# A Conformer branch layer, forward and backward: stores and loads moved from SyncE's DMA queue to GpSimd's and ScalarE's

## The chip, the cores and the metric
The kernel runs as one launch on one core of a Trainium2 chip. The time is the device time of the core in microseconds. The engines are named as in the profile: PE (TensorE matmul) with PEld (its weight load), DVE (VectorE), ACT (ScalarE), POOL (GpSimd) and SP (SyncE, which computes nothing here and issues DMAs).

## The reference
The layer has an attention branch and a local branch over x of shape (2, 4000, 144) in bfloat16. The kernel must return the output and the gradients of x and of all seven weights for a given grad_out.

```
xa = layernorm(x);  q, k, v = split(xa @ w_qkv)
p  = softmax(q k^T / sqrt(144));  glob = (p @ v) @ w_att_out
u, g = split(gelu(xa @ w_mlp_in));  g = layernorm(g)
gc = depthwise conv of g over time, 5 taps (dw_csgu)
loc = (u * gc) @ w_mlp_out
m = concat(glob, loc);  m = m + depthwise conv of m, 5 taps (dw_merge)
out = x + m @ w_merge
returns: out, and the gradients of x, w_qkv, w_att_out, w_mlp_in,
         dw_csgu, w_mlp_out, dw_merge, w_merge
```

## The kernel before
A batch of 4000 tokens is held as 125 partitions by 32 blocks, token = partition * 32 + block, so that there are 64 row tiles of 125 tokens in the two batches. Weights are folded together at the start (the head), so the attention works with rows of xa instead of q, k and v.

**Attention.** `phase_att` goes over the 64 row tiles, several of them in flight. For row tile i, the query rows and the rows of the incoming gradient are projected and turned by a DMA transpose (`jit_tr`, qt<-qb, L1162). `quad` makes the scores S and the products dP against all 4000 tokens of the batch, 1000 columns at a time (L1181, L1188). The scores go to Pbuf with a running minimum of their negative (DVE, L1203) and through the exponential (ACT, L1209); dP is copied to Sbuf by ACT (L1219) and multiplied by P on DVE (L1220). Both are transposed by DMA, half a row tile at a time: PT<-Pbuf at L1213 and ST<-Sbuf at L1408, all issued by SP. `Y_half` multiplies PT with xa (L1230, PE); ACT scales the result to yn (L1243), which is stored to DRAM (Yn_d, L1244), and GpSimd forms QBs (L1252), an operand of the matmuls X (L1325). `Z_half` does the same with ST (L1269) and stores zn (Zn_d, L1274); zn is also transposed (zt<-zn, L1281). The matmuls X sum the gradient of xa into acc on DVE (L1332). yn has two buffers and zn two.

**Local branch.** `local_units` does the local branch and its gradient per batch in small units woven into the attention. GpSimd computes a reciprocal root rsr (L596), which DVE uses at L611, and a product l_w (L677). The product u*g is stored to DRAM (ug_d, L658), and a few rows at the borders are spilled and read back (held, keep, ring, L533 to L644). Towards the end of the first batch `prep_late` loads x and grad_out of the second (L430 to L445), normalises them with statistics that GpSimd finishes (rstd_x, L458), and fills the rest of the operands (XR<-R, L504). Rows of the first batch that are needed again are spilled by `spill_xa0` (xa_d, L2006, called at L1499) and `spill_acc0` (acc_d, L2007, called at L1335).

**Merge and weight gradients.** `Merge` reads Yn_d, Zn_d and ug_d back, turns them by DMA transposes (L1672), computes the output in `out_g` (matmuls L1717 and L1719, the addition of x on DVE at L1720, a store) and the gradient of x in `dx_b` (DVE L1743, ACT L1744, GpSimd L1746, a store). The tiles o_ and dxo come from a pool with two buffers. `Final` computes the weight gradients and stores them.

**Who issues what.** `move` and `load_tok` split a transfer of 125 partitions into 112 and 13, so each is two DMAs (L47 and L48, L42 and L43). In the kernel before, SP issues nearly every DMA, 943 in the order lists; GpSimd issues 15 loads of weights into the operands of the end (L71, L100, L101), and ACT a few loads at the start.

**The order.** `Planner` records all instructions. `plan` (L1086) chains those of each engine in an order written out by hand: ORDER holds for each engine a list of numbers, one for each instruction or group of up to 16 alike (PE 1392 entries, DVE 2501, Activation 1668, Pool 379, SP 943). DMA issues are entries of the engine that issues them. An engine works strictly in this order, so an instruction that waits holds back all those behind it on its engine.

Of the kernel before, what the change touches and what calls it, by code (L numbers as in the profile page):

```python
# [411 lines left out]
def prep_late(k, W, b, S, es, pst):  # L412
# [15 lines left out]
    def start():  # L428
        nc.gpsimd.memset(S.xa_aug[:, :, D:D + 1], 1.0)
        nc.sync.dma_start(S.R[80:96, :], k.R0[80:96, :])  # L430
        nc.sync.dma_start(S.R[112:128, :], k.R0[112:128, :])
        nc.gpsimd.memset(halo_t[0:32, 0:2, :], 0.0)
        nc.gpsimd.memset(halo_t[96:PB, 2:4, :], 0.0)
        nc.sync.dma_start(halo_t[1:PB, 0:2, :], gv[0:PB - 1, NB - 2:NB, :])
        nc.sync.dma_start(halo_t[0:PB - 1, 2:4, :], gv[1:PB, 0:2, :])

    def load_x(g):
        if g < 4:
            load_tok(k, xin, 8 * g, xv, 8 * g, 8 * g + 8, nc.sync)

    def load_go(*qs):
        for q in qs:
            if q < 8:
                GQ[q] = sp.tile([PB, 4, D], BF, tag="gq", name="gq", bufs=4)
                load_tok(k, GQ[q], 0, gv, 4 * q, 4 * q + 4, nc.sync)  # L445
# [52 lines left out]
    def xar(g):  # L498
        pr = pst()
        for bi in range(8):  # L500
            nc.tensor.transpose(pr[0:112, bi, 0:PB], S.xa_aug[:, 8 * g + bi, 32:D], W.ident[0:PB, 0:PB])
        nc.vector.tensor_copy(v8(S.R, 8 * g, 8)[96:112], pr[96:112, :, 0:PB])
        for c in (2 * g, 2 * g + 1):
            nc.sync.dma_start(S.XR[32 * (c % 4):32 * (c % 4) + DR, (c // 4) * CH:(c // 4 + 1) * CH], S.R[96:112, c * CH:(c + 1) * CH])  # L504
# [17 lines left out]
def local_units(k, W, b, S, A, es, DHT, ps_w, gw):  # L522
# [10 lines left out]
    nc.sync.dma_start(held[1][PB - 1:PB].rearrange("p a b c -> p (a b c)"), k.zdram[0:1, 0:4 * D])  # L533
# [81 lines left out]
    def e_dgc(g):  # L615
# [5 lines left out]
        if g == NG2 - 1:  # L621
            nc.sync.dma_start(ring[1:PB, :, 0:2, :], t[0:PB - 1])
            nc.sync.dma_start(held[0][:], t)
        if g == 0:
            nc.sync.dma_start(held[1][0:PB - 1], t[1:PB])

    def e_hold():
        for i in range(2):
            nc.sync.dma_start(ring[:, :, 8 + 2 * i:10 + 2 * i, :], held[i][:])
        nc.sync.dma_start(hgr[0][:, :, 0:D], keep[0][:])  # L630
        nc.sync.dma_start(dugr[0][:], keep[1][:])
        nc.sync.dma_start(gpr[0][:], keep[2][:])
# [5 lines left out]
    def e_gp(g):  # L638
        nc.vector.tensor_tensor(sq[:], z_[:], a_[:], op=ALU.mult)
        nc.vector.tensor_tensor(gpr[new(g)][:], sq[:], q_[:], op=ALU.add)  # L640
        if g == NG2 - 1:
            nc.sync.dma_start(keep[0][:], hgr[new(g)][:, :, 0:D])
            nc.sync.dma_start(keep[1][:], dugr[new(g)][:])
            nc.sync.dma_start(keep[2][:], gpr[new(g)][:])  # L644
# [8 lines left out]
    def gc_unit(g):  # L653
# [4 lines left out]
        nc.sync.dma_start(S.ug_d[:, G2 * g:G2 * g + G2, :], ug[:])  # L658
# [113 lines left out]
class Planner:  # L772

    ORDER = {
# [1432 lines left out]
```

## Time and profile before

| | |
|---|---|
| runs (us) | 1182.25, 1186.67, 1194.44 |
| median | 1186.67 us |
| profiled execution | 1190.94 us |
| its span, first to last instruction | 1189.2 us |
| granted TensorE clock, mean | 0.992 |
| PE busy | 1134.5 us, 95% |
| DVE busy | 1021.0 us, 86% |
| ACT busy | 913.0 us, 77% |
| POOL busy | 228.1 us, 19% |
| share of the 16 DMA engines | 81.4% for SP's queue, 167 GB/s in the mean |

The profile is one execution. "Busy" counts instructions that compute; the time in which an engine issues a DMA isn't counted, so POOL's 19% and ACT's 77% leave out what they issue. A line such as "PE yz L1230 <- DMA PT<-Pbuf" says that PE, about to write yz at line 1230, waited for the DMA that fills PT from Pbuf. SPq, ACTq and POOLq are the queues of those engines, and a time beside a DMA issue there is how long the queue stood at it, which includes its wait for the source where the two aren't told apart. The span has five stages: the head up to about 60 us, attention of the first batch to 440, the change of batches to 530, attention of the second batch to 1045, and the merge with the weight gradients to the end.

### The profile page before, as it was taken

The page shows a single profiled execution, that of the slowest core. Times are in us where ns is not written, and L with a number is a line of the kernel's source. Part 1 is how long each engine was busy: PE and PEld are TensorE (multiplying, and loading weights), DVE is VectorE, ACT ScalarE, POOL GpSimd, SP SyncE. Part 2 cuts the span into 40 slices and gives each one's busy share as a digit, 9 for nine tenths or more (in the row PEclk, how much of TensorE's full clock was granted, in tenths as well). Part 3 has the DMA queues.
Part 4 walks back from the last instruction along what each step waited for, and adds up shares of the span by engine and source line. Part 5 has one row for each costly group of instructions (what it writes and reads, how often), then busy time and mean ns, then how long its engine had stood idle before and what let it go on. Part 6 is the DMA issues. An engine that isn't in the chain of part 4 may idle for free. (4 is left out here: it accounts for less than half of the span.)

```text
span 1189.2 us, 36104 instructions
## 1 busy us (share of the span) xinstructions
PE 1134.5 (95%) x14389; PEld 880.8 (74%) x14389; DVE 1021.0 (86%) x3043; ACT 913.0 (77%) x1662; POOL 228.1 (19%) x383
## 2 busy tenths in 40 slices
PE   6999999999999889999999999999999999998898
PEld 3667777777777667777676777777777776898887
DVE  8579999999999989778799999999999985676555
ACT  5999888888998766678898888888889766453252
POOL 7111112111112123200011111111111020023441
PEclk9999999999999999999999999999999999999989
DMA  3778888899898999778998988878989889857643
GB/s 106 165 167 167 160 165 176 177 159 182 167 185 165 166 172 203 167 149 170 205 193 160 160 171 161 185 157 172 167 175 165 174 167 181 205 148 185 157 124 97
DMA packets 673144, 198.43 MB, mean 167 GB/s; under 512 B 648915, under 2 KB 666889, under 8 KB 672955
## 3 DMA queue, kind: packets, MB, share of 16 engines
q1 hardware_dynamic: 671846, 194.74, 81.4%
q8 instruction: 112, 1.84, 0.7%
q0 software_dynamic: 592, 1.18, 0.4%
q14 instruction: 56, 0.46, 0.1%
q10 hardware_dynamic: 538, 0.21, 0.1%
HBM read 24.45 MB, written 17.85 MB: 36 GB/s over the span
## 5 line engine op out<-in xcount | busy, mean ns | idle before, releaser
L1203 DVE TENSOR_SCALAR_CACHE_REDUCE Pbuf<-ps 125x1000 bf16<-125x1000 f32 x256 | 306.3, 1197 | 47.0 <-PE ps L1188 37.5
L1219 ACT CAST Sbuf<-ps 125x1000 bf16<-125x1000 f32 x252 | 252.3, 1001 | 101.5 <-PE ps L1188 81.7
L1209 ACT ACTIVATE Pbuf<-Pbuf,nm 125x1000 bf16<-125x1000 bf16 x256 | 284.9, 1148 | 7.7 <-DVE nm L1205 7.4
L1325 PE MATMUL X<-QBs,Sbuf 125*128 125x144 bf16 x2048 | 282.8, 226 | 0.8 <-ACT QBs L1248 0.4
L1325 PE MATMUL X<-QBs,Pbuf 125*128 125x144 bf16 x2048 | 281.5, 226 | 1.0 <-POOL QBs L1252 0.6
L1181 PE MATMUL ps<-xaT_m,qt 128*128 128x500 bf16 x1024 | 262.3, 376 | 6.7 <-DVE Pbuf L1203 4.9
L1325 PEld LDWEIGHTS <-Sbuf 125*128 125x128 bf16 x2048 | 198.4, 98 | 18.7 <-issue 18.3
L1325 PEld LDWEIGHTS <-Pbuf 125*128 125x128 bf16 x2048 | 200.1, 98 | 2.1 <-issue 1.6
L1220 DVE TENSOR_TENSOR Sbuf<-Sbuf,Pbuf 125x1024 bf16<-125x1024 bf16 x252 | 172.0, 687 | 8.0 <-ACT Pbuf L1209 5.4
L1230 PE MATMUL yz<-xa_aug,PT 125*128 125x145 bf16 x2048 | 151.1, 228 | 14.1 <-DMA PT<-Pbuf 13.2
L1269 PE MATMUL yz<-xa_aug,ST 125*128 125x144 bf16 x2048 | 151.4, 229 | 4.9 <-DMA ST<-Sbuf 4.6
L1230 PEld LDWEIGHTS <-PT 125*128 125x128 bf16 x2048 | 131.7, 98 | 29.4 <-DMA PT<-Pbuf 18.7
L1181 PEld LDWEIGHTS <-qt 128*128 128x128 bf16 x1024 | 92.0, 98 | 70.6 <-issue 9.6
L1269 PEld LDWEIGHTS <-ST 125*128 125x128 bf16 x2048 | 133.2, 98 | 14.7 <-issue 8.0
L1252 POOL TENSOR_TENSOR QBs<-g,g 125x144 bf16<-125x144 f32 x64 | 35.7, 558 | 451.1 <-ACT g L1251 293.9
L1332 DVE TENSOR_TENSOR acc<-X,acc 125x432 f32<-125x432 f32 (+1 forms) x204 | 110.1, 547 | 13.7 <-PE X L1325 13.0
L1188 PEld LDWEIGHTS <-qt 16*128 16x128 bf16 x1024 | 26.4, 91 | 110.2 <-issue 110.2
L1188 PE MATMUL ps<-XR,qt 16*128 16x500 bf16 x1016 | 100.4, 380 | 0.0
L1744 ACT ACTIVATE t<-t,dx_c,rstd_x 125x144 f32<-125x144 f32 x64 | 28.6, 500 | 50.7 <-DVE t L1743 45.6
L649 DVE TENSOR_TENSOR l_prod<-ring,Wc 125x720 bf16<-125x720 bf16 x128 | 66.0, 535 | 0.2
L677 POOL TENSOR_SCALAR l_w<-ring,nc,c 125x144 f32<-125x144 bf16 x64 | 30.7, 485 | 176.1 <-DVE nc L673 86.1
L1614 PE MATMUL Hps<-Yg,go_h 125*128 125x144 bf16 x640 | 55.9, 229 | 1.5 <-DMA Yg<-ug_d 1.5
(558 smaller groups left out, 1941.7 us busy)
## 6 DMA issues: line engine op xcount, KB each, us to landing
Yn_d<-yn SPq DMA_DIRECT2D x64, 35.2 KB
Zn_d<-zn SPq DMA_DIRECT2D x64, 35.2 KB
ug_d<-ugr SPq DMA_DIRECT2D x32, 70.3 KB
PT<-Pbuf SPq DMA_TRANSPOSE x126
ST<-Sbuf SPq DMA_TRANSPOSE x126
acc_d<-acc SPq DMA_DIRECT2D x4, 504.0 KB
go_h<-in_grad_out_dram SPq DMA_DIRECT2D x8, 252.0 KB
Yg<-ug_d SPq DMA_DIRECT2D x8, 252.0 KB
```

Of the source, the lines that this page charges most:

```text
L649: nc.vector.tensor_tensor(prod[:, bi].rearrange("p a b -> p (a b)"), ring[:, a, p + bi:p + bi + 5, :].rearrange("p a b -> p (a b)"), W.Wc[ ...
L1181: mm = nc.tensor.matmul(pp[r // 2][:, r % 2, 0:CH], QT[i][:, 2 * h, :], bs(i)[0].xaT_m[:, c * CH:(c + 1) * CH], start=True, stop=False)
L1188: nc.tensor.matmul(pp[r // 2][:, r % 2, 0:CH], QT[i][rs, 2 * h + 1, :], xr, start=False, stop=True)
L1203: nc.vector.tensor_scalar(pv(pc(i, c2)), src, -1.0, 3.0e38, op0=ALU.mult, op1=ALU.min, accum_out=NM[i][:, c2:c2 + 1])
L1209: nc.scalar.activation(v, v, ACT.Exp, bias=NM[i][:, 4:5], scale=-1.0)
L1219: nc.scalar.copy(pv(sc(i, c2)), src)
L1220: nc.vector.tensor_tensor(sc(i, c2), sc(i, c2), pc(i, c2), op=ALU.mult)
L1230: nc.tensor.matmul(Yw, PT[0:PB, pos(i, j), :], S.xa_aug[:, j, 0:D + 1], start=(j == 0), stop=(j == NB - 1))
L1269: nc.tensor.matmul(Zw, ST[0:PB, j, :], S.xa_aug[:, j, 0:D], start=(j == 0), stop=(j == NB - 1))
L1325: nc.tensor.matmul(X[:, jj, :], l, r, start=(n_ == 0), stop=(n_ == len(ops) - 1))
L1332: nc.vector.tensor_tensor(av, X[0:PB, 0:nj, :], av, op=ALU.add)
L1614: nc.tensor.matmul(H[0:rows, a // 3, (a % 3) * D:(a % 3 + 1) * D], lhs, self.src[b][h][:, 2 + j, :], start=(n == 0 and a % 3 == 0), stop=( ...
```

## The change
324 of SP's 943 DMAs go to other queues.

- To GpSimd: the stores of yn, zn and u*g (64, 64 and 32), the spills of xa and acc and of the border rows and their reads, and the loads of `prep_late` for the second batch (x, grad_out, halo rows, rest rows). `spill_xa0` also becomes one DMA of 125 partitions instead of two, so 260 DMAs become 244.
- To ScalarE: the stores of the output (`out_g`) and of the gradient of x (`dx_b`), 32 tiles of two DMAs each.
- SP keeps the transposes, the loads of the merge, most of the head and the stores of weight gradients.
- All five order lists are written anew. PE keeps 1392 entries and DVE 2501; Activation has 1732, Pool 623, SP 619. The new places of PE's and DVE's entries lie near the old ones: in the mean a PE matmul moves by 14 places of 14389 and a DVE instruction by 5 of 2501.

```
 prep_late, start():
-        nc.sync.dma_start(S.R[80:96, :], k.R0[80:96, :])
+        nc.gpsimd.dma_start(S.R[80:96, :], k.R0[80:96, :])
...      (likewise S.R[112:128], both halo_t loads)
 prep_late, load_x / load_go:
-            load_tok(k, xin, 8 * g, xv, 8 * g, 8 * g + 8, nc.sync)
+            load_tok(k, xin, 8 * g, xv, 8 * g, 8 * g + 8, nc.gpsimd)
-                load_tok(k, GQ[q], 0, gv, 4 * q, 4 * q + 4, nc.sync)
+                load_tok(k, GQ[q], 0, gv, 4 * q, 4 * q + 4, nc.gpsimd)
...      (likewise the DMAs to S.XR)
 local_units:
-            nc.sync.dma_start(held[0][:], t)
+            nc.gpsimd.dma_start(held[0][:], t)
...      (likewise held, ring and keep, in all 11 lines)
-        nc.sync.dma_start(S.ug_d[:, G2 * g:G2 * g + G2, :], ug[:])
+        nc.gpsimd.dma_start(S.ug_d[:, G2 * g:G2 * g + G2, :], ug[:])
 Y_half, Z_half:
-        nc.sync.dma_start(S.Yn_d[:, j0, :], yn[:])
+        nc.gpsimd.dma_start(S.Yn_d[:, j0, :], yn[:])
-        nc.sync.dma_start(S.Zn_d[:, i % NB, :], zn[0:PB, 0:D])
+        nc.gpsimd.dma_start(S.Zn_d[:, i % NB, :], zn[0:PB, 0:D])
 Merge.out_g, Merge.dx_b:
-        move(nc.sync, tok_view(k.out0, b)[:, b0:b0 + GB, :], o_)
+        move(nc.scalar, tok_view(k.out0, b)[:, b0:b0 + GB, :], o_)
-        move(nc.sync, tok_view(k.out1, b)[:, bs, :], dxo)
+        move(nc.scalar, tok_view(k.out1, b)[:, bs, :], dxo)
 spills:
-    k.spill_xa0 = lambda j: move(nc.sync, k.xa_d[:, j:j + 2, :], ...)
-    k.spill_acc0 = lambda sl: move(nc.sync, k.acc_d[:, sl, :], acc[:, sl, :])
+    k.spill_xa0 = lambda j: nc.gpsimd.dma_start(k.xa_d[:, j:j + 2, :], ...)
+    k.spill_acc0 = lambda sl: move(nc.gpsimd, k.acc_d[:, sl, :], acc[:, sl, :])
 Planner.ORDER: the lists of PE, DVE, Activation, Pool and SP replaced
```

More of the change, by code (lines that the diff above doesn't have):

```diff
@@ L429, in start @@
         nc.gpsimd.memset(S.xa_aug[:, :, D:D + 1], 1.0)
-        nc.sync.dma_start(S.R[80:96, :], k.R0[80:96, :])
-        nc.sync.dma_start(S.R[112:128, :], k.R0[112:128, :])
+        nc.gpsimd.dma_start(S.R[80:96, :], k.R0[80:96, :])
+        nc.gpsimd.dma_start(S.R[112:128, :], k.R0[112:128, :])
         nc.gpsimd.memset(halo_t[0:32, 0:2, :], 0.0)
         nc.gpsimd.memset(halo_t[96:PB, 2:4, :], 0.0)
-        nc.sync.dma_start(halo_t[1:PB, 0:2, :], gv[0:PB - 1, NB - 2:NB, :])
-        nc.sync.dma_start(halo_t[0:PB - 1, 2:4, :], gv[1:PB, 0:2, :])
+        nc.gpsimd.dma_start(halo_t[1:PB, 0:2, :], gv[0:PB - 1, NB - 2:NB, :])
+        nc.gpsimd.dma_start(halo_t[0:PB - 1, 2:4, :], gv[1:PB, 0:2, :])
     def load_x(g):
         if g < 4:
-            load_tok(k, xin, 8 * g, xv, 8 * g, 8 * g + 8, nc.sync)
+            load_tok(k, xin, 8 * g, xv, 8 * g, 8 * g + 8, nc.gpsimd)
     def load_go(*qs):
@@ L503, in xar @@
         for c in (2 * g, 2 * g + 1):
-            nc.sync.dma_start(S.XR[32 * (c % 4):32 * (c % 4) + DR, (c // 4) * CH:(c // 4 + 1) * CH], S.R[96:112, c * CH:(c + 1) * CH])
+            nc.gpsimd.dma_start(S.XR[32 * (c % 4):32 * (c % 4) + DR, (c // 4) * CH:(c // 4 + 1) * CH], S.R[96:112, c * CH:(c + 1) * CH])
     P = [lambda: (start(), load_x(0), load_go(0, 1)), lambda: load_x(1), halos]
@@ L532, in local_units @@
     held = [tc.dram_tile([PB, 2, 2, D], BF, name="held%d_%d" % (b, i)) for i in range(2)]
-    nc.sync.dma_start(held[1][PB - 1:PB].rearrange("p a b c -> p (a b c)"), k.zdram[0:1, 0:4 * D])
+    nc.gpsimd.dma_start(held[1][PB - 1:PB].rearrange("p a b c -> p (a b c)"), k.zdram[0:1, 0:4 * D])
     keep = [tc.dram_tile([PB, G2, n], BF, name="keep%d_%d" % (b, i)) for i, n in enumerate((D, D, 2 * D))]
@@ L621, in e_dgc @@
         if g == NG2 - 1:
-            nc.sync.dma_start(ring[1:PB, :, 0:2, :], t[0:PB - 1])
-            nc.sync.dma_start(held[0][:], t)
+            nc.gpsimd.dma_start(ring[1:PB, :, 0:2, :], t[0:PB - 1])
+            nc.gpsimd.dma_start(held[0][:], t)
         if g == 0:
-            nc.sync.dma_start(held[1][0:PB - 1], t[1:PB])
+            nc.gpsimd.dma_start(held[1][0:PB - 1], t[1:PB])
     def e_hold():
         for i in range(2):
[L629 to L632, printed above, removed]
+            nc.gpsimd.dma_start(ring[:, :, 8 + 2 * i:10 + 2 * i, :], held[i][:])
+        nc.gpsimd.dma_start(hgr[0][:, :, 0:D], keep[0][:])
+        nc.gpsimd.dma_start(dugr[0][:], keep[1][:])
+        nc.gpsimd.dma_start(gpr[0][:], keep[2][:])
     def e_m(g):
@@ L641, in e_gp @@
         if g == NG2 - 1:
-            nc.sync.dma_start(keep[0][:], hgr[new(g)][:, :, 0:D])
-            nc.sync.dma_start(keep[1][:], dugr[new(g)][:])
-            nc.sync.dma_start(keep[2][:], gpr[new(g)][:])
+            nc.gpsimd.dma_start(keep[0][:], hgr[new(g)][:, :, 0:D])
+            nc.gpsimd.dma_start(keep[1][:], dugr[new(g)][:])
+            nc.gpsimd.dma_start(keep[2][:], gpr[new(g)][:])
     def taps(g, a):
@@ L774 @@
     ORDER = {
[54 rows of a table removed]
-        "DVE": [2, 1, 0, 3, 4, 8, 5, 11, 7, 9, 6, 10, 22, 12, 14, 15, 23, 16, 13, 17, 24, 25, 18, 43, 38, 42, 21, 20, 32, 19, 35, 33, 34, 36, 37, 26,
[101 rows of a table removed]
-        "Activation": [0, 1, 9, 4, 7, 10, 8, 12, 13, 14, 6, 15, 11, 16, 18, 34, 5, 35, 17, 3, 38, 19, 20, 21, 37, 40, 22, 43, 23, 2, 24, 28, 25, 29,
[65 rows of a table removed]
-        "Pool": [50, 0, 7, 4, 1, 11, 15, 8, 2, 9, 16, 3, 18, 6, 19, 47, 10, 41, 20, 17, 27, 26, 25, 24, 32, 21, 31, 33, 14, 37, 13, 38, 23, 12, 28,
[48 rows of a table removed]
[54 rows of a table added]
+        "DVE": [0, 2, 1, 3, 4, 8, 7, 5, 10, 11, 6, 9, 19, 12, 14, 15, 20, 16, 13, 17, 22, 25, 58, 42, 21, 24, 23, 37, 32, 38, 33, 35, 18, 34, 36, 26,
[101 rows of a table added]
+        "Activation": [1, 0, 4, 7, 9, 8, 10, 11, 15, 13, 14, 16, 5, 34, 12, 6, 17, 36, 18, 40, 37, 39, 19, 20, 22, 42, 21, 23, 2, 3, 38, 41, 24, 43,
[68 rows of a table added]
+        "Pool": [0, 6, 12, 1, 4, 8, 49, 15, 7, 2, 11, 10, 16, 18, 19, 41, 17, 25, 26, 24, 47, 32, 31, 33, 14, 38, 13, 37, 42, 39, 20, 9, 5, 35, 30,
[45 rows of a table added]
     }
@@ L2005 @@
     k.close_batch0 = es_x[0].close
-    k.spill_xa0 = lambda j: move(nc.sync, k.xa_d[:, j:j + 2, :], SS[0].xa_aug[:, j:j + 2, 0:D])
-    k.spill_acc0 = lambda sl: move(nc.sync, k.acc_d[:, sl, :], acc[:, sl, :])
+    k.spill_xa0 = lambda j: nc.gpsimd.dma_start(k.xa_d[:, j:j + 2, :], SS[0].xa_aug[:, j:j + 2, 0:D])
+    k.spill_acc0 = lambda sl: move(nc.gpsimd, k.acc_d[:, sl, :], acc[:, sl, :])
     A = K()
```

536 rows, old and new, of the table ORDER are left out of this document.

## The prediction
> **What bounds the kernel now.** The first view read is the page's table of engines with its line of DMA queues, then the table of windows by stage (columns: stretch, its length, then busy time and count of PE, weight load, DVE, ACT, POOL, then granted clock, DMA share, GB/s).
>
> ```profile
> span 1189.2 us, 36104 instructions
> PE 1134.5 (95%) x14389; PEld 880.8 (74%) x14389; DVE 1021.0 (86%) x3043; ACT 913.0 (77%) x1662; POOL 228.1 (19%) x383
> q1 hardware_dynamic: 671846, 194.74, 81.4%
> 60.00:440.00 380.00, 368.36 (x4608) 277.89 (x4606) 360.75 (x1075) 329.55 (x593) 62.23 (x96) 1.00 0.88 170
> 440.00:530.00 90.00, 85.76 (x1057) 65.04 (x1057) 71.05 (x202) 63.14 (x101) 20.33 (x37) 0.98 0.86 173
> 530.00:1045.00 515.00, 503.56 (x6352) 385.70 (x6351) 456.57 (x1274) 423.27 (x739) 71.51 (x118) 1.00 0.88 173
> 1045.00:1170.00 125.00, 112.30 (x1733) 108.36 (x1731) 81.19 (x327) 47.46 (x105) 46.79 (x75) 0.96 0.63 152
> 1170.00:1189.00 19.00, 14.72 (x203) 13.11 (x200) 9.80 (x44) 3.42 (x14) 1.27 (x1) 0.96 0.37 97
> ```
>
> PE sets the end. It is idle 1189.2 - 1134.5 = 54.7 us, and the change removes no matmul, so 54.7 us is all that it could ever win. By stage the idle time is 11.6 us in the first attention stretch (380 - 368.36), 4.2 in the change of batches, 11.4 in the second attention stretch, 12.7 in the merge, 4.3 at the end; the head has the remaining 10 or so. In the first attention stretch DVE is 95% busy (360.75 of 380), so a delay on DVE has only 19 us of room there; in the second the room is 58 us. The next view is what PE waited for (total, times, longest).
>
> ```profile
> PE yz L1230 <- DMA PT<-Pbuf: 13.2, 16, 2.9
> PE pm L1538 <- DVE o__20883 L1720: 4.7, 1, 4.7
> PE yz L1269 <- DMA ST<-Sbuf: 4.6, 4, 2.3
> PE X L1325 <- POOL QBs L1252: 0.6, 1, 0.6
> ```
>
> The transposes that SP issues cost PE 13.2 + 4.6 = 17.8 us, so SP's queue matters. Whether the DMAs that leave SP are the reason is read from what SP's own queue waited for, and from one gap.
>
> ```profile
> SPq L1213 <- ACT Sbuf L1219: 68.2, 37, 4.3
> SPq L1408 <- PE yz L1230: 40.1, 28, 2.7
> SPq L1408 <- DVE Sbuf L1220: 30.5, 25, 3.2
> L1213 SPq DMA_TRANSPOSE PT<-Pbuf x126: 1484/1778/4284, 31.1 to 1013.2; - x126
> 381.79 3.71 SPq L1213 DMA_TRANSPOSE PT<-Pbuf  x1
> 389.15 1.19 PE L1230 MATMUL yz<-xa_aug,PT 125*128 125x145 bf16 x16 [1.63 <-DMA PT<-Pbuf]
> ```
>
> These three waits of SP sum to 138.8 us. The transpose at 381.79 takes 3.71 us to issue where the median is 1.78: SP stood at it until its source was ready, and PE's 1.63 us gap at 389.15 followed. SP was early, not late. In the other gaps on PT and ST that I followed it was mostly so. That reading carries the forecast.
>
> **What leaves SP.** 324 of its 943 DMAs leave. The largest families, with the issue time of one (min, median, max in ns):
>
> ```profile
> L1244 SPq DMA_DIRECT2D Yn_d<-yn x64: 250/440/544, 60.2 to 1047.7; - x64
> L1274 SPq DMA_DIRECT2D Zn_d<-zn x64: 250/463/514, 74.6 to 1048.5; - x64
> L658 SPq DMA_DIRECT2D ug_d<-ugr x32: 267/410/497, 125.1 to 989.5; - x32
> L47 SPq DMA_DIRECT2D xa_d<-xa_aug x16: 343/573/1687, 29.0 to 359.9; - x16
> L47 SPq DMA_DIRECT2D out_dram<-dxo x16: 316/343/581, 1082.7 to 1184.2; - x16
> ```
>
> That is 64 x 0.440 = 28.2, 64 x 0.463 = 29.6, 32 x 0.410 = 13.1 and 16 x 0.573 = 9.2 us of SP's time, and about 64 x 0.37 = 24 us for all output stores (two DMAs for each of 32). The bytes and the 16 DMA engines stay: their share is 0.88 in the attention stretches before and, as an estimate, after. Freed issue time wins only where a transpose stood behind one of these DMAs with its source ready. The bounds are 0 and the whole 17.8 us; I take **-1 us**, since the followed gaps are nearer to nothing.
>
> **What POOL takes on.** 244 issues. The nearest rows are POOL's own DMA issues in this trace, in a quiet stretch and, the two with times, amid attention work with DVE running:
>
> ```profile
> L100 POOL DMA_DIRECT2D XR<-in_w_qkv_dram x1 | 0.6, 563 | 0.0
> 667.24 0.79 POOL L71 DMA_DIRECT2D R<-sWr_d  x1
> 699.95 0.64 POOL L71 DMA_DIRECT2D R<-sWr_d  x1
> L596 POOL TENSOR_TENSOR rsr<-ve,mhalf x32: 695/711/1197, 74.2 to 925.2; 125x2 f32<-125x2 f32 x32
> L677 POOL TENSOR_SCALAR l_w<-ring,nc,c x64: 452/462/962, 103.8 to 970.0; 125x144 f32<-125x144 bf16 x64
> L1252 POOL TENSOR_TENSOR QBs<-g,g 125x144 bf16<-125x144 f32 x64 | 35.7, 558 | 451.1 <-ACT g L1251 293.9
> DVE rsr L611 <- POOL rsr L596: 1.1, 4, 0.3
> ```
>
> At 0.6 us each the issues are 244 x 0.6 = 146 us, and POOL goes from 228 to 374 of 1189 us: far from full. Capacity is not the question; order is. A store that waits on POOL's queue for yn, zn or ug holds back what stands behind it: rsr (32 times) and l_w (64 times), for which DVE waits, and QBs (64 times), for which PE's X matmuls wait. QBs has 451.1 us of idle time before it and cost PE 0.6 us in all, so I price it at nothing; if that cover were gone it would be 64 x 0.6 = 38 us. rsr costs DVE 1.1 us now, so its hand-offs are close. Between 0 and half of the 96 hand-offs late by one issue (48 x 0.6 = 29 us of DVE's time) I take **+1.5 us**, near the present 1.1: in the new order most stores stand where their source is already written.
>
> Against this speaks a rule of the Trainium skill, "SBUF — State Buffer", sections "SBUF: two separate sides" and "Who interferes with whom": a DMA that GpSimd issues can't have its descriptors written while DVE holds the shared port in one of its fast modes, and took about 3.1 us instead of 0.62 beside a DVE copy. The two rows amid DVE work show 0.79 and 0.64, so the trace bears out little of it; by the page's figure 244 issues would be an estimated 756 us.
>
> **The change of batches.** The second batch's x, gradient and halo loads go from SP to POOL, ahead of POOL's own statistics:
>
> ```profile
> 440.80 0.50 SPq L43 DMA_DIRECT2D xa_aug<-in_x_dram  x1
> 451.35 1.65 POOL L458 TENSOR_TENSOR rstd_x<-pve,mhalf 125x8 f32<-125x8 f32 x1 [4.25 <-DVE pve L457]
> ```
>
> Some 14 loads come in a burst, 14 x 0.6 = 8.4 us of POOL. On SP the same loads were interleaved with transposes over more than 20 us, so the first load may even come earlier, and POOL idled 4.25 us before its first statistic. Bounds: -4.2 (the stage's whole PE idle time) to +8.4; I take **+0.5**.
>
> **The tail.** In the merge SP handles transposes, loads and stores in one row, and the output tiles are two deep.
>
> ```profile
> 1118.40 0.44 DVE L1720 TENSOR_TENSOR o__20768<-po,xo 125x288 bf16<-125x288 f32 x1
> 1121.21 1.33 SPq L47 DMA_DIRECT2D out_dram<-o__20768  x1
> 1124.43 0.46 DVE L1720 TENSOR_TENSOR o__20828<-po,xo 125x288 bf16<-125x288 f32 x1 [3.86 <-DMA out_dram<-o__20768]
> 1179.33 0.46 DVE L1720 TENSOR_TENSOR o__22386<-po,xo 125x288 bf16<-125x288 f32 x1 [1.01 <-PE po L1719]
> 1183.75 0.40 SPq L48 DMA_DIRECT2D out_dram<-o__22386  x1
> 1185.32 0.82 DVE L1720 TENSOR_TENSOR o__22496<-po,xo 125x288 bf16<-125x288 f32 x2 [2.53 <-DMA out_dram<-o__22386]
> 0.74 0.41 ACTq L148 DMA_DIRECT2D raw<-in_w_qkv_dram  x1
> ```
>
> The tile o__20768 was written at 1118.84 and its store issued from 1121.21 on, 2.4 us late; o__22386 was written at 1179.79 and its second store issued at 1183.75, 4 us late. DVE paid 3.86 and 2.53 us for a free tile, and the second of these lies on the very end. From ACT's queue, where an issue took 0.41 us and which is 38% busy in the merge (47.46 of 125) and 18% at the end, the store can follow its tile at once. ACT pays 64 x 0.41 = 26 us for it in 144 us of stage with about 93 idle, so it stays beside PE's work; if that cover were gone, all 26 us would count. Bounds: 0 to -11 (3.86 + 2.53 + the 4.7 that PE stood at L1538 for an output tile). I take **-4.5**: the 2.53 whole and half of 3.86.
>
> **Sum.** -1 + 1.5 + 0.5 - 4.5 = -3.5. The profiled execution took 1190.94 us (1189.2 of span and 1.7 around it); minus 3.5 is 1187.4. It stood 4.3 above the median of 1186.67, so the forecast for the median is **1183 us**. 1% of the time, 12 us, is about what a measurement of this kernel can tell from no change.
>
> **Rivals.**
> *Hidden queueing on SP* (0.27): the transposes did stand behind stores, and the new order uses the room. Two thirds of the 17.8 us go, plus the tail's 4.5: 1187 - 16.4 = 1170. For it: 17.8 us is the largest group of PE's waits. Against it: SP waited 138.8 us for sources.
> *POOL's order* (0.20), slower: rsr and l_w come late because a store ahead of them on POOL waits for its source. Price: 29 us of DVE's time, of which DVE's room swallows a third: 1187 + 20 = 1207. It decides once more than a third of the 96 hand-offs find a store in front. For it: DVE at 95% in the first stretch, and 1.1 us of rsr waits now. Against it: POOL's 81% idle time.
> *Long issues on POOL* (0.04), slower: an issue beside DVE stretches as DVE's own t did beside POOL:
>
> ```profile
> L1743 DVE SCALAR_TENSOR_TENSOR t<-xa0r,dx_s,acc x32: 346/357/2355, 1112.9 to 1170.1; 125x144 f32<-125x144 bf16 x32
> ```
>
> From 0.36 to 2.36, so by 2.0 us. Then 244 x 2.6 = 634 us of POOL, and 48 late hand-offs at 2.6 are 125 us of DVE's time, about 50 of them beyond DVE's 77 us of room: 1237. The skill's rule above is this one; the 0.64 and 0.79 speak against it.
> *Late loads of the second batch* (0.07), slower: the burst on POOL delays rstd and then the first projections by two bursts' length, 15 us net: 1202.
> *Nothing moves* (0.08): the shift of issue time hides nothing and costs nothing, 1187. The Trainium skill, "DMA: Bandwidth & Descriptors", section "Issuing engines are not separate DMA queues", says that DMAs of all queues end on the same 16 engines and that issuing from several saves only the sequencer's time; no row here decides how much that is worth.
>
> **How the numbers follow.** The forecast has 0.34. Faster by over 1%: the first rival, 0.27. Within 1%: the forecast and no move, 0.42. Slower: 0.20 + 0.04 + 0.07 = 0.31. The likeliest case alone spans 1176 to 1192. The range goes from 1166, below the first rival, to 1210, above POOL's order; long issues and extremes are left out.
>
> **What would show it.** Right: PE's wait for PT stays within some us of 13.2, POOL's issues near 0.6 us with POOL at 30 to 33% busy counting them, DVE's waits for out_dram gone from L1720, no new PE wait on QBs. Wrong: DVE waiting for rsr or l_w by tens of us; PE's PT wait below 5 or above 25; ACT's t late at L1744 because an issue waits for its tile; a gap of PE around 445 to 470 on the second batch's loads.

## The result, and the profile after
The changed kernel takes 1229.38 us in the median (1224.7 to 1235.96) against 1185.49 for the kernel before: a ratio of 1.036 with a 95% interval of 1.029 to 1.044. The forecast was 1183 with a range of 1166 to 1210, so the change is slower where no change was forecast. It also lies past the 1207 of the likelier slower rival; only "Long issues on POOL" (1237, chance 0.04) had a time so high.

The page of the changed kernel, and its table of windows, with the stretches moved to the stages of this execution (columns as in the prediction):

```profile
span 1233.8 us, 36193 instructions
PE 1151.9 (93%) x14389; PEld 892.1 (72%) x14389; DVE 1021.9 (83%) x3043; ACT 918.3 (74%) x1662; POOL 382.9 (31%) x627
q1 hardware_dynamic: 630452, 174.33, 73.1%
q0 software_dynamic: 11152, 17.06, 6.3%
60.00:460.00 400.00, 379.27 (x4662) 284.97 (x4659) 367.37 (x1086) 334.35 (x599) 125.47 (x188) 0.98 0.86 163
460.00:560.00 100.00, 88.97 (x1066) 67.69 (x1064) 69.29 (x193) 62.23 (x98) 46.77 (x85) 0.93 0.86 154
560.00:1090.00 530.00, 507.89 (x6333) 387.05 (x6331) 457.53 (x1272) 421.66 (x737) 134.08 (x221) 0.98 0.87 169
1090.00:1233.80 143.80, 127.29 (x1896) 121.52 (x1893) 87.07 (x370) 52.60 (x119) 48.08 (x75) 0.95 0.56 140
```

The span grew by 44.6 us (1233.8 - 1189.2). DVE and ACT do the same work in the same time. POOL's busy time grew by 154.8 us with 244 more instructions (x383 to x627), which are its DMA issues: unlike ACT's, POOL's share on the page counts them, and so did its 19% before. PE's idle time grew from 54.7 to 81.9 us, by 27.2; and PE's busy time grew by 17.4, with the same 14389 matmuls, because the granted clock fell from 0.992 to 0.974 in the mean. The two belong together, as a table of ten-microsecond windows around two gaps shows:

```profile
80.00:90.00 10.00, 8.65 (x102) 6.01 (x99) 9.54 (x31) 10.00 (x23) 5.44 (x7) 1.00 1.00 172
90.00:100.00 10.00, 6.55 (x54) 4.51 (x51) 4.04 (x9) 5.19 (x11) 6.10 (x8) 0.66 0.91 173
100.00:110.00 10.00, 8.90 (x119) 7.13 (x117) 9.42 (x38) 9.73 (x18) 5.96 (x10) 1.00 0.67 147
590.00:600.00 10.00, 5.27 (x30) 3.15 (x29) 2.00 (x6) 4.39 (x9) 2.87 (x6) 0.68 1.20 206
```

In the windows with gaps of 3.45 and 4.37 us the clock is 0.66 and 0.68, and at 100 us it is back at 1.00: a gap is paid twice, once as idle time and once in slow matmuls behind it. The Trainium skill, "TensorE: Matmul & The Clock Gate", section "Why this matters for your kernels", says that gaps over about 3 us throw the clock to half speed. These rows agree, but the bound isn't sharp here: behind gaps of 2.05 us (at 253) and 2.48 us (at 405.5) the clock is 0.83 in the windows 254 to 264 and 404 to 414.

PE's waits (total, times, longest), and some of the gaps in PE's, ACT's and POOL's timelines:

```profile
PE yz L1230 <- DMA PT<-Pbuf: 14.8, 15, 2.2
PE yz L1269 <- DMA ST<-Sbuf: 13.6, 7, 3.5
PE ps L1181 <- DMA qt<-qb: 6.0, 2, 5.0
PE po L1719 <- DMA VUsl<-VUs_d: 5.8, 2, 4.2
PE X L1325 <- ACT acc L1330: 4.4, 1, 4.4
PE X L1325 <- POOL QBs L1252: 2.5, 4, 0.9
93.89 1.40 PE L1269 MATMUL yz<-xa_aug,ST 125*128 125x144 bf16 x10 [3.45 <-DMA ST<-Sbuf]
593.96 0.28 PE L1325 MATMUL X<-QBs,Sbuf 125*128 125x144 bf16 x1 [4.37 <-ACT acc L1330]
593.39 0.52 ACT L1330 COPY acc<-X 125x432 f32<-125x432 f32 x1 [4.83 <-issue]
583.78 0.57 POOL L47 DMA_DIRECT2D acc_d<-acc  x1
640.05 0.60 PE L1181 MATMUL ps<-xaT_m,qt 128*128 128x500 bf16 x1 [5.04 <-DMA qt<-qb]
```

The wait for PT hardly moved (13.2 to 14.8); that for ST tripled (4.6 to 13.6), that for a transpose qt grew from 0.9 to 6.0, and two causes are new: loads of VUsl in the merge, and ACT's first write to acc. The last looks like a wait for the spill of acc that GpSimd issues at 583.78, since ACT overwrites what that spill reads: by the completion events of the trace it lands at 593.32, 9.0 us after the end of its issue, and ACT starts at 593.39.

Matmul by matmul the loss isn't spread: the changed kernel is 6 us late at the 1080th, 17 at the 5040th, 28 at the 5400th, 42 at the 7560th, and stays between 40 and 50 from there on.

### The profile page after: what moved, and what is told of

Its sections match the earlier page's. It is cut to its first block, busy times and chain, and to the rows that moved or that the text cites. A ratio compares the mean times of both kernels' runs of the same rounds, so it can differ in the third digit from the quotient of the medians.

```text
span 1233.8 us, 36193 instructions
## 1 busy us (share of the span) xinstructions
PE 1151.9 (93%) x14389; PEld 892.1 (72%) x14389; DVE 1021.9 (83%) x3043; ACT 918.3 (74%) x1662; POOL 382.9 (31%) x627
## 3 DMA queue, kind: packets, MB, share of 16 engines
q0 software_dynamic: 11152, 17.06, 6.3%
## 4 chain that ended last, share of the span: by engine, by line
PE 64%; DMA 15%; DVE 10%; ACT 7%; issue 2%; POOL 1%; SPq 1%; ACTq 0%; DVEq 0%; POOLq 0%
PE X L1325 16%; PE ps L1181 13%; PE yz L1269 8%; PE yz L1230 8%; DMA PT<-Pbuf 7%; PE ps L1188 5%; DMA ST<-Sbuf 4%; DVE Pbuf L1203 3%; PE Hps L1614 3%; ACT Pbuf L1209 2%; PE po L1717 2%; DMA out_dram<-dxo 2%; ACT Sbuf L1219 1%; DVE Sbuf L1220 1%; PE pd L606 1%
## 5 line engine op out<-in xcount | busy, mean ns | idle before, releaser
L1203 DVE TENSOR_SCALAR_CACHE_REDUCE Pbuf<-ps 125x1000 bf16<-125x1000 f32 x256 | 306.1, 1196 | 58.5 <-PE ps L1188 48.1
L1181 PE MATMUL ps<-xaT_m,qt 128*128 128x500 bf16 x1024 | 268.3, 383 | 13.7 <-DVE Pbuf L1203 6.1
L1269 PE MATMUL yz<-xa_aug,ST 125*128 125x144 bf16 x2048 | 155.2, 231 | 14.4 <-DMA ST<-Sbuf 13.6
L1230 PE MATMUL yz<-xa_aug,PT 125*128 125x145 bf16 x2048 | 152.6, 229 | 16.3 <-DMA PT<-Pbuf 14.8
L1269 PEld LDWEIGHTS <-ST 125*128 125x128 bf16 x2048 | 136.9, 100 | 24.6 <-DMA ST<-Sbuf 16.0
L677 POOL TENSOR_SCALAR l_w<-ring,nc,c 125x144 f32<-125x144 bf16 x64 | 33.6, 529 | 100.7 <-DVE nc L673 50.9
```

The source lines that it names most:

```text
L1181: mm = nc.tensor.matmul(pp[r // 2][:, r % 2, 0:CH], QT[i][:, 2 * h, :], bs(i)[0].xaT_m[:, c * CH:(c + 1) * CH], start=True, stop=False)
L1203: nc.vector.tensor_scalar(pv(pc(i, c2)), src, -1.0, 3.0e38, op0=ALU.mult, op1=ALU.min, accum_out=NM[i][:, c2:c2 + 1])
L1230: nc.tensor.matmul(Yw, PT[0:PB, pos(i, j), :], S.xa_aug[:, j, 0:D + 1], start=(j == 0), stop=(j == NB - 1))
L1269: nc.tensor.matmul(Zw, ST[0:PB, j, :], S.xa_aug[:, j, 0:D], start=(j == 0), stop=(j == NB - 1))
```

## Experiments: the queues under the old order, and the reverse
The change is two things, other queues and another order. Each experiment keeps the code of before or after, changes which engine issues a family of DMAs, and gives every engine the list of one order; a moved DMA stands in its new engine's list at the time at which it was issued in the trace of that order's kernel. Three families: 160 small stores (yn, zn, u*g), 64 output stores, and 84 bulky transfers (spills of xa, acc and border rows with their reads; the second batch's loads). Each xa spill is one DMA, except in new_order, where it is two as in the kernel before.

```
old_order:  queues of after                     ORDER of before
new_order:  queues of before                    ORDER of after
bulk_sp:    k.spill_xa0, k.spill_acc0, held/ring/keep, prep_late:
            nc.gpsimd -> nc.sync                ORDER of after
small_sp:   S.Yn_d, S.Zn_d, S.ug_d:
            nc.gpsimd -> nc.sync                ORDER of after
```

> The changed queues with the order of before: PE's and DVE's lists are those of before, and the 308 moved DMAs stand in GpSimd's and ScalarE's lists where SyncE issued them in the trace of before. Theory Q (the moves themselves cost the time: transfers on GpSimd's queue share the 16 DMA engines with the transposes and land late, so PE pauses and its clock drops): 1215 to 1235 us. Theory O (the new order costs the time, the queues nothing): 1180 to 1192. If it is the bursts in which GpSimd issues the second batch's loads and the spills, not the queue as such, this spaces them out as before: 1190 to 1210.

> The queues of before with the new order: PE's and DVE's lists are the new ones, and the 324 DMAs stand in SyncE's list where GpSimd and ScalarE issued them in the trace of after. Theory Q: 1180 to 1195. Theory O: 1220 to 1235.

> The changed kernel, but the 84 bulky transfers (spills of xa, acc and the border rows with their reads, and the loads of the second batch) are back on SyncE, at the times at which GpSimd issued them; the 160 stores of yn, zn and u*g stay on GpSimd. Theory Q in the form that the bulky transfers do it (three of the large gaps of PE stand beside them): 1185 to 1205. Rival S (the 160 small stores do it): 1220 to 1235. Theory O: 1220 to 1235.

> The changed kernel, but the 160 stores of yn, zn and u*g are back on SyncE, the bulky transfers stay on GpSimd. Theory Q in the bulky form: 1215 to 1235. Rival S: 1185 to 1205. Theory O: 1220 to 1235.

Measured: old_order 1211.77, ratio 1.025 (1.020 to 1.029); new_order 1239.21, 1.048 (1.043 to 1.052); bulk_sp 1220.49, 1.030 (1.026 to 1.035); small_sp 1236.17, 1.046 (1.041 to 1.051). Neither theory holds alone, rival S is refuted by small_sp, and the two parts don't simply add. With the kernel before and the changed one (1.036) these runs make a square. The moves cost 2.5% under the old order; under the new order the changed queues are faster than the old ones (1.036 against 1.048). The new order costs 4.8% with the old queues and 1.2% with the queues that it was written for (1.036 against 1.025). In both pairs the intervals just overlap, while no execution of one kernel lies among those of the other. Under the new order, with the bulky transfers on SyncE in both, 224 more DMAs on SyncE cost 1.8% (new_order against bulk_sp); the places that they were given in SyncE's list may have a part in it. Whether the bulky transfers alone are better on SyncE there (1.030), and the small stores on GpSimd (1.046 without), the intervals around 1.036 leave open.

## Experiments: which of the moves
```
old_bulk:       queues of before, the 84 bulky: nc.sync -> nc.gpsimd      ORDER of before
old_small:      queues of before, the 160 small: nc.sync -> nc.gpsimd     ORDER of before
old_out:        queues of before, the 64 output stores: nc.sync -> nc.scalar
old_prep:       only prep_late's 36 -> nc.gpsimd
old_acc:        only the 8 of k.spill_acc0 -> nc.gpsimd
old_spill:      only the 40 of k.spill_xa0, held, ring, keep -> nc.gpsimd
old_bulk_act:   the 84 bulky: nc.sync -> nc.scalar
old_small_out:  the 160 -> nc.gpsimd and the 64 -> nc.scalar
```

> The order of before, and only the 84 bulky transfers (spills of xa, acc and border rows with their reads, loads of the second batch) on GpSimd; all other DMAs are on SyncE as before. With all moves the order of before took 1212 us against 1185. If the bulky transfers carry that: 1200 to 1212. If the 160 small stores do: 1183 to 1192.

> The order of before, and only the 160 stores of yn, zn and u*g on GpSimd. If the bulky transfers carry the 27 us: 1183 to 1192. If the small stores do: 1200 to 1212.

> The order of before, and only the 64 output stores on ScalarE. The prediction's term for this part, -4.5 us, says 1178 to 1183; if ACT pays for the 64 issues after all: 1186 to 1196.

Measured: old_bulk 1208.41, 1.017 (1.013 to 1.021); old_small 1187.13, 1.001 (0.998 to 1.003); old_out 1186.72, 1.000 (0.998 to 1.002). Under the old order the bulky transfers carry most of the loss (1.7% of old_order's 2.5%), and each of the two other families is free by itself. The trace of old_bulk shows one place where time goes, at the change of batches: DVE's and PE's timelines, SP's, what SP waited for there (460 to 480 us), then DVE's waits in old_bulk and, last, in the kernel before.

```profile
476.21 0.52 DVE L450 BATCH_NORM_STATS2 pst<-xa_aug 125x6 f32<-125x144 bf16 x2 [6.64 <-DMA xa_aug<-in_x_dram]
477.89 0.99 PE L1181 MATMUL ps<-xaT_m,qt 128*128 128x500 bf16 x2 [6.31 <-DVE Pbuf L1203]
468.51 9.45 SPq L1213 DMA_TRANSPOSE PT<-Pbuf  x2
SPq L1213 <- ACT xaT_m L496: 3.9, 1, 3.9
DVE pst L450 <- DMA xa_aug<-in_x_dram: 8.7, 4, 6.6
DVE pst L450 <- DMA xa_aug<-in_x_dram: 0.7, 2, 0.5
```

DVE, which works in order, waits 6.64 us for a part of x; the row minimum L1203 that PE needs stands behind it, and PE stops for 6.31. The two transposes that SP issued meanwhile took 9.45 us where two take 3.6 by the median of the kernel before; the profile puts up to 3.9 of it to SP's wait for ACT, and in the stretches of 2 us from 468 to 476 the DMA engines show a share of 0.97 to 1.53. That transposes and the load hinder each other on the 16 DMA engines is the likely reading; no run separates it. By the completion events of the trace, the eight loads of x land 2.95 us (median) after the end of their issue on SyncE's queue, 4.1 in old_bulk, and 9.3 in the changed kernel, where GpSimd issues six of them and four of grad_out within 8 us. There the pair of PT transposes at 461.7 took 13.62 us to issue, of which up to 7.3 are SP's wait for ACT (waits of SP, 455 to 480 us):

```profile
461.70 13.62 SPq L1213 DMA_TRANSPOSE PT<-Pbuf  x2
SPq L1213 <- ACT qb L1158: 7.3, 2, 5.1
xa_aug<-in_x_dram POOLq DMA_DIRECT2D x4, 252.0 KB, 10.2
```

> The order of before, and only the 36 loads and copies of the second batch's preparation on GpSimd; the rest on SyncE. All 84 bulky transfers on GpSimd cost 21 us, and its profile loses 10.7 us between the PE matmuls 5040 and 5400, where DVE waits 6.6 us for a load of x, and 11 more between 6480 and 7560, where acc is spilled. If the loads carry the first part: 1195 to 1199. If the cost comes only from all transfers together: 1186 to 1190.

> The order of before, and only the 8 spills of acc on GpSimd. If they carry the second part of the loss of the bulky transfers (matmuls 6480 to 7560): 1194 to 1199. If not: 1185 to 1189.

> The order of before, and only the 40 spills of xa and of the border rows, with their reads, on GpSimd. The 36 loads of the second batch cost 0.6% there and the 8 spills of acc 0.5%, all 84 together 1.7%. If the parts add up: 0.6%, so about 1195 us against 1188. If the rest is contention among them: 1186 to 1190.

Measured: old_prep 1197.18, 1.006 (1.003 to 1.010); old_acc 1193.69, 1.005 (1.002 to 1.009); old_spill 1195.44, 1.008 (1.005 to 1.011). The three add up to 1.9%, which is within the interval of the 1.7% for all together: each family has its own price. How the two families of spills pay it isn't shown. Old_prep's ten executions lie between 1185 and 1201; in the profiled one, of 1190, the loads of x land 3.3 us (median) after the end of their issue, and DVE hardly waits for them. It waits longer for GpSimd's statistics rstd_x, 2.9 us against 0.6 in the kernel before (waits of DVE in old_prep, then GpSimd's timeline):

```profile
DVE pst L450 <- DMA xa_aug<-in_x_dram: 1.4, 3, 1.0
DVE pnm L462 <- POOL rstd_x L458: 2.9, 2, 2.2
490.94 0.24 POOL L478 COPY pgo_r<-gq 125x64 bf16<-125x64 bf16 x1 [3.36 <-DMA gq<-in_grad_out_dram]
492.91 1.67 POOL L458 TENSOR_TENSOR rstd_x<-pve,mhalf 125x8 f32<-125x8 f32 x1
```

The late one of these statistics stands on GpSimd behind a copy that waits for a load of grad_out, so it is held by a landing too.

> The order of before, and the 84 bulky transfers on ScalarE's queue instead of GpSimd's, at the same times. If GpSimd's way of making DMAs (descriptors written in software, few large packets) makes them land late: 1186 to 1194, with ACT paying for at most 84 issues. If any second queue beside that of the transposes does it: 1203 to 1213.

Measured: 1199.8, 1.011 (1.005 to 1.016), between the two theories. DVE waits for x here too, less (old_bulk_act, waits of DVE):

```profile
DVE pst L450 <- DMA xa_aug<-in_x_dram: 4.6, 2, 3.9
```

ScalarE's queue, which the profile lists as hardware_dynamic like SyncE's, costs 1.1% where GpSimd's (software_dynamic) costs 1.7%; the intervals overlap. What the two have in common is that a load no longer takes its turn among the transposes, which makes that a likely cause, not a shown one: the 84 issues also stand among ACT's own instructions here, and no run tells that price apart. Nor was what is GpSimd's own taken apart: in the changed kernel its 11152 packets hold 1.5 KB each in the mean (17.06 MB), those of q1 0.28 KB, and its issues are longer.

> The order of before with the 160 small stores on GpSimd and the 64 output stores on ScalarE, all bulky transfers on SyncE: the part of the moves that cost nothing each by itself. If SyncE's issue time matters once enough of it is freed: 1176 to 1182. If not: 1185 to 1190. It is also the old-order partner of the run with the bulky transfers back on SyncE (1220), so their difference is the price of the new order with the same queues.

Measured: 1188.94, 1.002 (0.999 to 1.005). Under the old order, freeing SyncE of 224 issues wins nothing. And bulk_sp, with the same queues and the new order, took 1.030: with these queues the new order costs about 2.8%, some 33 us. Like every kernel here that mixes an order with other queues, bulk_sp includes the places that the returned DMAs were given in SyncE's list.

## Experiments: the new order
```
new_fix2:      after, list of SP: one qt<-qb moved ahead of one ST<-Sbuf; 8 loads VUsl<-VUs_d together
after_xa:      after, list of Pool: the 16 spills of xa at their old times
old_xanew:     queues and order of before, 16 spills of xa at the new times
new_then_old:  bulk_sp, new order up to 440 us, then that of before
old_then_new:  bulk_sp, order of before up to 424 us, then the new one
```

> The changed kernel with two places of SyncE's list mended: one transpose qt<-qb stands ahead of the waiting transpose ST<-Sbuf that it stood behind (PE's gap of 5.0 us at 640), and the eight loads of VUsl stand together at the place of the first (PE's gaps of 1.6 and 4.2 us at 1118 to 1124). If such places in the new order are a cause: 7 to 14 us less than the changed kernel's 1229, so 1215 to 1222, and those two gaps gone. If PE then waits for something else at the same places: 1226 to 1232.

Measured: 1226.58, 1.033 (1.029 to 1.036), next to the changed kernel's 1.036 and in the second range: PE waits for something else at about the same places. The gap at qt stayed, 3.98 us against 5.04, so the transpose was not held up by its place on SP alone; and behind the mended loads stood the next late thing, by the look of it: DVE, ahead of L1720, waits 10.8 us at L1729 for a load (the profile names Zn<-Zn_d), and the loads of the merge now stand behind all eight (timeline and waits of PE in new_fix2):

```profile
628.86 0.60 PE L1181 MATMUL ps<-xaT_m,qt 128*128 128x500 bf16 x2 [3.98 <-DMA qt<-qb]
PE po L1717 <- DVE o__20448 L1720: 7.3, 1, 7.3
```

> The changed kernel with the 16 spills of xa alone put back to the times that they had before (spread from 52 to 368 us; in the changed kernel 7 stand between 51 and 132 us beside the spills of the border rows, and 4 between 380 and 409 us beside their reads). If such bunches of bulky transfers are what the new order costs in the first attention stretch (its profile lost 8 us there by matmul 1440 and 4 between 4320 and 5040): 1214 to 1221. If the new order's cost lies elsewhere: 1226 to 1232.

> The order and the queues of before, with the 16 spills of xa (each one DMA) put in SyncE's list where the new order has them in time, in bunches around 80 to 130 and 370 to 400 us. If bunches of bulky transfers cost PE time on any queue: 1193 to 1199. If not: 1184 to 1190.

Measured: after_xa 1235.59, 1.040 (1.035 to 1.045), if anything slower; old_xanew 1189.96, 1.002 (0.999 to 1.005). The theory that the new order's bunches of xa spills do it falls on both sides.

> The queues of the run with the bulky transfers back on SyncE (1220 us under the new order); the new order up to 440 us of the changed kernel's trace, and from there on the order of before. If the new order costs time at single places all along (its profile lost 9.6 us by matmul 5040 and 16 after it): 1196 to 1202. If the loss sits in the second part alone: 1186 to 1190. If in the first alone: 1214 to 1220.

> The queues of the run with the bulky transfers back on SyncE (1220 us under the new order), the order of before up to 424 us of its trace and the new one from there on. The reverse split took 1201 against 1187. If the two parts of the new order add up: 1187 + (1220 - 1201) = 1206, so 1202 to 1210. If the new order is only bad as a whole: 1214 to 1220.

Measured: new_then_old 1201.0, 1.012 (1.006 to 1.018); old_then_new 1202.39, 1.013 (1.009 to 1.018). The two halves add up to about the whole, which fits a price that is a sum of single places along the program. The same gap turns up under the new order with every choice of queues (timelines of PE in new_order, bulk_sp, small_sp), and in none of the kernels with the old order (old_order and old_bulk have one of 2.9 and 2.4 us a row tile earlier):

```profile
631.77 1.01 PE L1181 MATMUL ps<-xaT_m,qt 128*128 128x500 bf16 x2 [6.05 <-DMA qt<-qb]
618.41 1.01 PE L1181 MATMUL ps<-xaT_m,qt 128*128 128x500 bf16 x2 [5.44 <-DMA qt<-qb]
631.92 0.87 PE L1181 MATMUL ps<-xaT_m,qt 128*128 128x500 bf16 x3 [4.21 <-DMA qt<-qb]
```

What in the order makes such places stays open; lists of single engines weren't exchanged between the two orders. The fastest of all kernels run take as long as the kernel before; none beats it.

## Why the prediction was wrong, point by point
**"What leaves SP", -1 us: right under the order of before.** There old_small_out frees SP of 224 issues and changes nothing (1.002). SP was early at its transposes, as its waits said. Under the new order it doesn't carry over: the same 224 on SP cost 1.8% (new_order against bulk_sp).

**"What POOL takes on": right for the small stores, wrong for the bulky ones.** An issue of a small store costs 0.53 to 0.55 us in the median, rsr and l_w hold DVE up by little, and the stores cost nothing (1.001, against +1.5 us forecast). Rows of the changed kernel:

```profile
L1244 POOL DMA_DIRECT2D Yn_d<-yn x64: 531/547/905, 49.2 to 1085.4; - x64
L2006 POOL DMA_DIRECT2D xa_d<-xa_aug x16: 1166/1209/1537, 51.5 to 409.0; - x16
  DVE rsr L611: 1.2, 1
  DVE l_dd L682: 1.3, 2
```

The rule of the Trainium skill on GpSimd's descriptors ("SBUF — State Buffer", section "SBUF: two separate sides", 3.1 us beside a DVE copy) doesn't show here: no store of yn took over 0.91 us with DVE 83% busy, though no run tells how much of DVE's work is in such a fast mode. The failed step is "244 x 0.6": the size was right (154.8 us for 244 issues), but it priced each DMA by its issue and none by its landing. The bulky transfers had no price for that, and they cost 1.7% together; the spills among them, which had no price at all, cost 0.5% (acc) and 0.8% (the others). Two late landings are seen to hold up PE: that of x in old_bulk, and by its times that of an acc spill in the changed kernel. For the border and xa spills the way stays open.

**"The change of batches", +0.5 us: wrong in size and cause.** It measured 0.6%, some 7 us, within the bounds given (to +8.4), which is luck: the bound was worked out from the time that GpSimd takes to issue the burst. What is seen to be late is a landing: of x in old_bulk and the changed kernel, of grad_out, ahead of rstd_x, in old_prep. Whether these waits make up the 0.6% stays open.

**"The tail", -4.5 us: wrong.** old_out measured 1.000. DVE still waits for the same stores, whose buffer numbers are 16 lower here (waits of DVE and the end of ACT's queue in old_out):

```profile
DVE o__20812 L1720 <- DMA out_dram<-o__20752: 4.3, 1, 4.3
DVE o__22480 L1720 <- DMA out_dram<-o__22370: 2.2, 1, 2.2
1179.62 0.38 ACTq L47 DMA_DIRECT2D out_dram<-o__22370  x1
1182.87 0.25 ACT L1953 COPY o<-fpt 5x128 bf16<-5x128 bf16 x1 [5.51 <-PE fpt L1950]
1182.88 0.32 ACTq L48 DMA_DIRECT2D out_dram<-o__22370  x1
```

The second half of the tile's store stands behind an ACT instruction that waits 5.51 us for PE. The forecast let the store "follow its tile at once" and forgot that ACT works in order too. In the changed kernel the stretch from the merge to the end is 143.8 us long, against 144 before.

**The new order, priced at nothing: the second failed step.** The forecast took the small moves in the lists as neutral: it has no term for them, and says of the new order only that "most stores stand where their source is already written". At equal queues the new order costs 1.2% with the changed queues, 2.8% with the bulky transfers on SyncE and 4.8% with the queues of before. Its gaps are of another kind than the forecast looked for: PE waits 5.0 us for a transpose qt, 4.2 for a load of VUsl and 4.4 behind the spill of acc. Why the order brings them stays open.

**Rivals.** The likelier slower one named POOL's order and hand-offs; those were not late. "Long issues on POOL" came nearest in time, by luck: the issues took 0.63 us in the mean, not 2.6. "Late loads of the second batch" (0.07) came nearest in kind: rstd_x does come late in old_prep, but behind a landing and not behind the burst of issues. "Hidden queueing on SP" is refuted under the order of before. None had the clock: of the 44.6 us of span, 17.4 are longer busy time of PE at the lower clock.

## What to carry to other kernels
Price a DMA that changes queues by when it lands and by what it meets, not by its issue alone: under the order of before, moving 84 bulky transfers off the queue of the transposes cost 1.7%, moving 224 small ones was free. An order written out by hand belongs to the queues that it was written for: here the same order cost 1.2% or 4.8%, by the queues. Measure it apart from the change that it came with, by a run with the old order and the new queues and one the other way round. And where an engine's clock falls behind a gap, add that to the gap.

## What was not expected of the hardware
Two PT transposes that take 3.6 us to issue took 9.45 and 13.62 while loads of 252 KB were under way on another queue; SP's wait for their sources is at most 3.9 and 7.3 of that. A load of 252 KB from there landed 10.2 us after its issue, in the median of four. Two gaps of PE, of 3.45 and 4.37 us, went with a granted clock of 0.66 and 0.68 in the ten microseconds around them, and gaps of 2.05 and 2.48 us with 0.83.
